# Turning z(1)'s third piece and loading v(1)'s first piece one stage earlier

## The chip, the cores and the metric

The kernel runs on one core of a Trainium2 chip. The metric is the device time of one execution in microseconds. The span in the profile, from the first to the last instruction, is about 1.8 us shorter than that time (916.8 for an execution of 918.57). A timed set is five rounds of one kernel beside the kernel before, on the same chip. Four such sets are used, called the first to the fourth; the second to the fourth ran on three different chips.

In the views, PE is TensorE's matmuls, PEld its weight loads, DVE is VectorE, ACT ScalarE, POOL GpSimd, and SPq the DMA queue that SyncE fills. A transfer has landed when its data is in place. The DMA share is the time of all packets over that of 16 engines; it passes 1 in some stretches here (1.19 from 98 to 104 us in the first trace).

## The reference, cut to what matters

```python
batch, seq, d_model, d_qk, d_ff = 8, 3072, 256, 64, 1024
scores = (1 / seq) * z @ z.T              # per batch
attn   = relu(scores) ** 2
x      = u * (attn @ v)                   # gated attention unit
out    = max(x @ w1, x @ w2) @ w_out      # feed-forward with maxout
```

## The kernel before

Each batch is cut into six groups of 512 rows, and two groups are a couple. For a couple, TensorE runs a stage of products of attention blocks with v. Score pairs for later couples are interleaved with those products. While a couple's gates are prepared, TensorE runs the feed-forward stage ("ff") of the couple before it. All matmuls are bf16.

Scores need z transposed and doubled. A batch's z comes in three pieces of 1,024 rows. Each is loaded (`load_z`), doubled by two VectorE copies, and transposed by a DMA (`turn_z`):

```python
def turn_z(b, piece):
    t = zpool.tile([P, 2 * G, 2, dqk], bf16, name="zd")
    for h in range(2):
        nc.vector.tensor_copy(t[:, :, h, :], zn[b, piece])              # L141, DVE
    nc.sync.dma_start_transpose(                                        # L142, SP queue
        zT[:, ds(z_at(b, piece * 2 * G), 2 * G), :], t.rearrange("p t h d -> p (t h d)"))

def load_v(b, piece, lo=0, n=2 * G, held=False):
    # [cut: takes a tile of the pool of five]
    nc.gpsimd.dma_start(out=t[:, ds(lo, n), :], in_=...)                # L156, POOL queue, 512 KB
```

The place of these calls is set by hand. In batch 0's last couple (`i == 2`, 96 steps, with 22 score pairs of batch 1 interleaved) a plan names the step of each. The ff stage ahead of it takes tasks at fixed places, six in each of its two groups:

```python
# ahead of the couple: the ff stage of batch 0's first couple
second(PLAIN // 2 - 2, [lambda: turn_z(1, 1), lambda: None] + tasks)    # tasks: two gates

if i == 2:
    plan = [
        (2, load_u, 0, 4), (6, load_u, 0, 5),
        (14, turn_z, 1, 2),            # the third piece of z(1)
        (24, load_v, 1, 0),            # the first piece of v(1)
        (52, turn_u, 0, 4), (58, turn_u, 0, 5),
        (len(steps), load_v, 1, 1),
    ]
# the loop over steps (cut)
mm = nc.tensor.matmul(a.out(acc[name]), w()[rows], a.moving(rows, j), ...)   # L880, products
```

The score matmuls are at L210, block transposes (SP queue) at L262, u's transposes (SP queue) at L186.

## Time and profile before

| | before |
|---|---|
| median of the first three timed executions | 914.85 us (914.19 to 915.84) |
| the execution that was profiled | **918.57 us**, span 916.8 us |
| TensorE busy in it | 904.3 us |

The head of the page of the kernel before says that TensorE fills the span:

```profile
span 916.8 us, 19322 instructions
## 1 busy us (share of the span) xinstructions
PE 904.3 (99%) x7518; PEld 519.9 (57%) x7566; DVE 707.8 (77%) x1077; ACT 603.6 (66%) x1192; POOL 105.8 (12%) x199
```

The list of waits of PE (who waited for what: total us, times, longest) leads with the transposed z:

```profile
PE s_ps L210 <- DMA zT<-zd: 2.0, 1, 2.0
PE acc L581 <- DVE blk L557: 1.2, 1, 1.2
```

The timeline of PE shows where (start, duration, what, how many; in brackets the idle time before it and what ended it). Score pairs normally start 1.08 us apart with 8 products between them, 1.29 us with 10:

```profile
97.06 0.38 PE L210 MATMUL s_ps<-zT 64*128 64x512 bf16 x2
97.28 1.03 PE L880 MATMUL acc<-blk,v_sb 64*128 64x512 bf16 x8
100.35 0.39 PE L210 MATMUL s_ps<-zT 64*128 64x512 bf16 x2 [2.04 <-DMA zT<-zd]
100.58 2.04 PE L880 MATMUL acc<-blk,v_sb 64*128 64x512 bf16 x10
102.41 0.64 PE L210 MATMUL s_ps<-zT 64*128 64x512 bf16 x2
```

The pair at 100.35 is the couple's fifteenth, the first that reads z(1)'s third piece. Ten products after it take 2.04 us instead of 1.24. The timeline of the SP queue, and the view of the tile zT in this stretch, show how late the piece was:

```profile
85.76 3.67 SPq L262 DMA_TRANSPOSE blk<-blk  x1
89.53 1.25 SPq L142 DMA_TRANSPOSE zT<-zd  x1
90.87 9.11 SPq L186 DMA_TRANSPOSE uT<-un  x2
...
DMA to landing us min/median/max: 10.8/10.8/10.8
```

Just before its issue, the timeline of POOL has the load of v(1) that flies beside it:

```profile
89.26 0.53 POOL L156 DMA_DIRECT2D v_sb<-in_v_dram  x1 [4.58 <-PE acc L880]
```

Stretches of the same trace (us, then the busy time of PE, PEld, DVE, ACT and POOL, the granted TensorE clock, the DMA share and GB/s) show spare DMA time ahead of the couple, and the halt, with the lowered clock after it:

```profile
74.00:82.00 8.00, 7.95 (x59) 5.46 (x60) 0.00 (x0) 5.10 (x10) 1.09 (x2) 1.00 0.67 110
90.00:98.00 8.00, 8.00 (x78) 3.54 (x74) 4.86 (x8) 7.58 (x16) 0.00 (x0) 1.00 1.14 107
98.00:104.00 6.00, 3.96 (x24) 1.39 (x22) 1.59 (x3) 2.57 (x6) 0.00 (x0) 0.74 1.19 200
```

### The profile page before, as it was taken

How to read it: one execution, taken by the hardware profiler on the slowest of the kernel's cores; microseconds unless marked ns; L12 is line 12 of the kernel's file. 1: busy time of each engine (PE TensorE's matmuls, PEld its weight loads, DVE VectorE, ACT ScalarE, POOL GpSimd, SP SyncE). 2: the span in 40 equal slices, each digit the busy share in tenths (PEclk: the TensorE clock that was granted, in tenths of full speed). 3: DMA queues.
4: the chain of work that ended last, by engine and by line, in shares of the span. 5: the costliest groups of instructions: out<-in, count | busy, mean ns of one | idle time of the engine just before them, and what ended most of it. 6: DMA issues, size and time to landing. Idle time of an engine off the chain costs nothing.

```text
span 916.8 us, 19322 instructions
## 1 busy us (share of the span) xinstructions
PE 904.3 (99%) x7518; PEld 519.9 (57%) x7566; DVE 707.8 (77%) x1077; ACT 603.6 (66%) x1192; POOL 105.8 (12%) x199
## 2 busy tenths in 40 slices
PE   8999999999999999999999999999999999999998
PEld 4456365564655655655556656466465564655655
DVE  6772526888997799987998979979799788995640
ACT  6797756567666676766666666766766667673445
POOL 3101020110101101101011111010110110100000
PEclk9999999999999999999999999999999999999999
DMA  9998999999899897998979999899979999697201
GB/s 184 188 192 159 164 192 137 185 171 162 142 173 187 161 162 139 192 187 141 175 124 207 172 147 168 141 199 161 163 149 162 181 165 174 131 178 140 80 24 69
DMA packets 379499, 145.07 MB, mean 158 GB/s; under 512 B 358160, under 2 KB 362640, under 8 KB 379408
## 3 DMA queue, kind: packets, MB, share of 16 engines
q1 hardware_dynamic: 356960, 91.27, 62.3%
q0 software_dynamic: 22448, 52.57, 29.7%
q8 instruction: 59, 0.97, 0.4%
q14 instruction: 32, 0.26, 0.1%
HBM read 59.77 MB, written 25.17 MB: 93 GB/s over the span
## 4 chain that ended last, share of the span: by engine, by line
PE 96%; DMA 1%; DVE 1%; issue 0%; ACT 0%; ACTq 0%; DVEq 0%
PE acc L880 44%; PE o_ps L462 18%; PE d_ps L439 18%; PE s_ps L210 7%; PE o_ps L453 5%; PE acc L278 4%; DMA zT<-zd 1%; DVE blk L231 1%; PE acc L581 0%; ACT r_sb L223 0%; DVE r_sb L221 0%; PE w2o_ps L673 0%; ACT zT L128 0%; PE tpw L658 0%; DVE xT L423 0%
## 5 line engine op out<-in xcount | busy, mean ns | idle before, releaser
L880 PE MATMUL acc<-blk,v_sb 64*128 64x512 bf16 x2304 | 454.6, 378 | 0.0
L223 ACT ACTIVATE r_sb<-s_ps 128x512 bf16<-128x512 f32 (+3 forms) x668 | 334.3, 558 | 129.1 <-PE s_ps L210 87.3
L880 PE MATMUL acc<-blk,vt 64*128 64x512 bf16 x1440 | 346.7, 376 | 0.0
L880 PEld LDWEIGHTS <-v_sb 64*128 64x128 bf16 x2304 | 178.5, 94 | 139.6 <-issue 7.7
L231 DVE TENSOR_TENSOR blk<-r_sb 128x1024 bf16<-128x1024 bf16 x257 | 173.1, 690 | 109.5 <-ACT r_sb L223 108.4
L446 ACT ACTIVATE g_sb<-d_ps 128x512 bf16<-128x512 f32 x384 | 193.3, 627 | 27.9 <-PE acc L880 17.1
L462 PE MATMUL o_ps<-w_out_sb,g_sb 128*128 128x256 bf16 x1536 | 175.5, 273 | 0.0
L439 PE MATMUL d_ps<-xT,w_sb 128*128 128x512 bf16 x720 | 167.9, 379 | 2.6 <-issue 0.2
L880 PEld LDWEIGHTS <-vt 64*128 64x128 bf16 x1440 | 132.6, 94 | 59.9
L462 PEld LDWEIGHTS <-g_sb 128*128 128x128 bf16 x1536 | 150.3, 98 | 17.4
L474 ACT COPY o_sb<-o_ps 128x512 f32<-128x512 f32 (+1 forms) x98 | 56.4, 578 | 132.1 <-PE o_ps L462 132.1
L210 PE MATMUL s_ps<-zT 64*128 64x512 bf16 (+3 forms) x676 | 126.3, 359 | 2.7 <-DMA zT<-zd 2.0
L439 PEld LDWEIGHTS <-w_sb 128*128 128x128 bf16 x768 | 73.2, 98 | 89.9 <-issue 10.3
L762 DVE TENSOR_TENSOR h_sb<-h_sb,acc 128x512 f32<-128x512 f32 x160 | 104.3, 683 | 23.3 <-ACT h_sb L766 16.0
L475 POOL DMA_DIRECT2D out_dram<-o_sb x88 | 48.2, 547 | 500.7 <-ACT o_sb L474 500.7
L330 DVE TENSOR_TENSOR blk<-blk,blk 128x2048 bf16<-128x2048 bf16 x60 | 73.2, 1219 | 7.3 <-DMA blk<-blk 7.2
L334 DVE TENSOR_TENSOR blk<-blk,blk 128x2048 bf16<-128x2048 bf16 x60 | 73.5, 1225 | 2.0
L777 DVE TENSOR_TENSOR blk<-blk,blk 128x2048 bf16<-128x2048 bf16 x60 | 73.0, 1219 | 0.0
L338 DVE TENSOR_TENSOR blk<-blk,blk 128x2048 bf16<-128x2048 bf16 x60 | 69.8, 1218 | 0.0
L423 DVE SCALAR_TENSOR_TENSOR xT<-h_sb,uT 128x512 bf16<-128x512 f32 x96 | 62.0, 685 | 5.5 <-PE o_ps L453 3.9
L229 DVE TENSOR_TENSOR blk<-r_sb 128x512 bf16<-128x512 bf16 (+3 forms) x162 | 46.3, 323 | 21.2 <-ACT r_sb L223 20.2
L210 PEld LDWEIGHTS <-zT 64*128 64x128 bf16 x676 | 35.7, 94 | 41.2 <-DMA zT<-zd 2.5
(50 smaller groups left out, 322.8 us busy)
## 6 DMA issues: line engine op xcount, KB each, us to landing
out_dram<-o_sb POOLq DMA_DIRECT2D x88, 256.0 KB, 3.6
un<-in_u_dram POOLq DMA_DIRECT2D x48, 256.0 KB, 6.2
v_sb<-in_v_dram POOLq DMA_DIRECT2D x21, 512.0 KB, 7.8
blk<-blk SPq DMA_TRANSPOSE x239, 5.1
zn<-in_z_dram POOLq DMA_DIRECT2D x21, 128.0 KB, 3.7
v_sb<-in_v_dram POOLq DMA_DIRECT2D x6, 256.0 KB, 7.4
out_dram<-o_sb SPq DMA_DIRECT2D x6, 256.0 KB, 2.0
blk<-in_moe_w_dram POOLq DMA_DIRECT2D x2, 512.0 KB, 7.2
```

The costliest lines, as they stand in the source:

```text
L210: nc.tensor.matmul(s_ps[h][:, lo[h] :], zT[rows, z_at(b, blk * G + tiles[h]), :], zT[rows, q + lo[h] // P : q + G, :].rearrange("p t c -> ...
L223: nc.scalar.activation(o, s, AF.Relu)
L231: nc.vector.tensor_mul(a[:, k : k + 2, :], r, r)
L330: nc.vector.tensor_add(*alike(f["S1"], f["A21"], f["A22"]))
L334: nc.vector.tensor_sub(*alike(f["S2"], f["S1"], f["A11"]))
L338: nc.vector.tensor_sub(*alike(f["S3"], f["A11"], f["A21"]))
L439: nc.tensor.matmul(d_ps, w15_sb[:, kc, ts(nb, P)], xT[:, kc, :], start=(kc == 0), stop=(kc == KD - 1),)
L446: nc.scalar.activation(g_sb[:, nb, :], d_ps, AF.Relu)
L462: nc.tensor.matmul(o_ps[t // 2][:, t % 2, :], g_sb[:, nb, ts(t, P)], w_out_sb[:, nb, :], start=False, stop=(nb == KF - 1 and t % 2 == 1),)
L762: nc.vector.tensor_add(out, a, b_)
L777: nc.vector.tensor_sub(f["A12"].ap, f["A12"].ap, f["S2"].ap)
L880: mm = nc.tensor.matmul(a.out(acc[name]), w()[rows], a.moving(rows, j), start=name not in opened, stop=left[name] == 0,)
```

## The change

Both calls move from the couple into the ff stage ahead of it, so that the transpose has landed long before its use and the load of v starts at 75.67 us instead of 89.26.

```diff
-        second(PLAIN // 2 - 2, [lambda: turn_z(1, 1), lambda: None] + tasks)
+        second(
+            PLAIN // 2 - 2,
+            [lambda: turn_z(1, 1)]
+            + tasks
+            + [lambda: turn_z(1, 2)]
+            + [lambda: None] * 2
+            + [lambda: load_v(1, 0)],
+        )
@@ plan of i == 2
-                    (14, turn_z, 1, 2),
-                    (24, load_v, 1, 0),
```

## The prediction

> **What bounds the kernel.** TensorE: 904.3 of 916.8 us busy (page, part 1), and 96% of the chain that ended last is PE. The list of waits gives PE almost nothing to wait for: one wait of 2.0 us on the transposed z (`zT<-zd`), the longest on PE, and scraps of 1.2 us and less, all outside the region of the change. So the whole kernel can win little more than what hangs on that one wait.
>
> **The wait.** In batch 0's last couple (PE from 82 us) 22 score pairs of batch 1 are interleaved; from the fifteenth on they read z(1)'s third piece. In the timeline its doubling copies run on DVE at 85.6, its transpose is issued by SP only at 89.53, behind a 3.67 us block transpose, and lands 10.77 us later; transposes of z take 3.7 us at the median of all 21. It flies beside a 512 KB load of v(1) (issued 89.26, 7.6 us) and u's transposes (from 90.87); the windows show DMA share 1.14 in 90 to 98. PE has done fourteen pairs and stands until 100.35.
>
> **Its full cost.** Score starts before and after: 97.06, then 100.35, 102.41, 104.42. Elsewhere in the same couple such distances are 1.08 us (8 products between) or 1.29 (10). 97.06 to 104.42 is 7.36 us against 1.08 + 1.29 + 1.08 = 3.45: lost 3.91 us. Of it 2.2 us is standing still; 1.7 us is slow matmuls after it (pairs at about 0.42 us apart instead of 0.216, granted clock 0.74 in 98 to 104, 1.00 around it). [...]
>
> **What the change does.** No work is added or removed. By the built order, the two copies (0.49 us on DVE) go ahead of the first block product of that couple, into a stretch (72.0 to 83.9 us) where DVE idles 11.9 us. The transpose follows directly on that of the second piece, so SP issues it at about 74.5 to 76. The load of v goes between the output writes of the first couple's two ff groups; it no longer waits for PE, so starts near 75.7 instead of 89.3. In 74 to 82 the DMA share is 0.67, so there is room. Estimate: with landing between the 3.7 median and 10.8 worst, zT is there by 79 to 87 us, at least 11 us before its use at 98. z(0) is no longer read then, so it is not held up. The second piece (issued 72.4, 6.2 us) may land a few us later, but is first used at 89.1.
>
> **On the critical path:** all 3.91 us, since PE is the chain here and further PE waits on DMA do not follow in the trace. Lighter DMA at 89 to 98 gives nothing more directly: u's transposes come earlier, but nobody waits for them.
>
> **Predicted:** 914.85 - 3.9 = 910.95 us; range 909.7 to 912.9. Faster by over 2%: 0.005; within: 0.99; slower: 0.005.
>
> **Would show it right:** no PE wait on zT; clock 1.00 through the couple; all later PE work shifted about 3.9 us earlier, span near 913; third zT transpose issued near 75. **Wrong:** a PE wait at the fifteenth pair, or slow matmuls, remain.
>
> **What could spoil it:** with PE 3.9 us earlier, block transposes (DMA share about 1.1 to 1.2 from 98 to 128) or u's transposes may turn late for the next stages, handing some back; the early v load may delay the second zT piece past 85 us, moving the stall forward; run spread (914.19 to 915.84) is itself 1.6 us.

## The result, and the profile after

| | before | after |
|---|---|---|
| median of five timed executions | 914.85 us (914.19 to 915.84) | 914.91 us (914.45 to 915.31) |
| ratio of the mean times, 95% interval | | 1.000 (0.9986 to 1.0015) |
| profiled execution | 918.57 us, span 916.8 | 915.31 us, span 913.5 |

A ratio here is the mean time of one kernel's fast runs over that of the other's of the same rounds, so it is not quite the ratio of the medians.

The two profiles differ by 3.3 us in span, the timed executions by nothing. The predicted 910.95 us was wrong, and so was its range of 909.7 to 912.9.

In the trace, nearly every step went as predicted. The head of the page after, and the first line of PE's waits, where the transpose of z (`zT<-zd`) no longer stands. (Each trace also has waits of 0.9 us or less at the start of the kernel for parts of zT that ACT or DVE write; they are left out where this text says "no wait on zT".)

```profile
span 913.5 us, 19368 instructions
...
PE acc L278 <- DVE blk L231: 1.3, 4, 0.6
```

The timelines of POOL, SP and PE after:

```profile
75.67 0.55 POOL L156 DMA_DIRECT2D v_sb<-in_v_dram  x1
...
73.14 4.83 SPq L142 DMA_TRANSPOSE zT<-zd  x2
85.74 5.05 SPq L262 DMA_TRANSPOSE blk<-blk  x1
...
97.09 0.38 PE L210 MATMUL s_ps<-zT 64*128 64x512 bf16 x2
97.30 1.03 PE L885 MATMUL acc<-blk,v_sb 64*128 64x512 bf16 x8
98.17 0.38 PE L210 MATMUL s_ps<-zT 64*128 64x512 bf16 x2
98.38 1.24 PE L885 MATMUL acc<-blk,v_sb 64*128 64x512 bf16 x10
```

The two transposes of z on the SP queue, and the window that showed the halt:

```profile
L142 SPq DMA_TRANSPOSE zT<-zd x2: 1371/2362/3353, 73.1 to 76.6; - x2
DMA to landing us min/median/max: 7.7/8.1/8.5
...
98.00:104.00 6.00, 6.00 (x60) 2.68 (x57) 3.69 (x6) 5.79 (x12) 0.00 (x0) 1.00 1.15 212
```

The third piece is issued at 76.6 and landed by 85.1, 13 us before the fifteenth pair at 98.17. The second piece landed by about 81, before its use at 89.1. From 82 to 112 us PE has no gap, the clock is 1.00, and the next ff stage starts at 107.54 instead of 111.42.

So the trace loses a 3.9 us delay (3.3 us are left of it at the end of the span) and the timed executions lose nothing. Either the trace of before was not of an ordinary execution, or the time came back in a way the trace does not show. That was the question for the experiments.

### The profile page after: what moved, and what is told of

It is laid out like the page before. It is cut to its first block, busy times and chain, and to the rows that moved or that the text cites. A ratio compares the mean times of both kernels' runs of the same rounds, so it can differ in the third digit from the quotient of the medians.

```text
span 913.5 us, 19368 instructions
## 1 busy us (share of the span) xinstructions
PE 905.2 (99%) x7566; PEld 519.5 (57%) x7566; DVE 707.8 (77%) x1077; ACT 603.5 (66%) x1192; POOL 105.4 (12%) x199
## 4 chain that ended last, share of the span: by engine, by line
PE 94%; DVE 3%; DMA 2%; ACT 1%; issue 1%; SPq 0%; POOL 0%; ACTq 0%; DVEq 0%; POOLq 0%
PE acc L885 43%; PE d_ps L439 18%; PE o_ps L462 18%; PE s_ps L210 7%; PE o_ps L453 4%; PE acc L278 4%; DMA uT<-un 2%; DVE blk L231 1%; ACT r_sb L223 0%; DVE xT L423 0%; DVE blk L330 0%; DVE blk L338 0%; PE acc L581 0%; DVE blk L334 0%; DVE r_sb L221 0%
## 5 line engine op out<-in xcount | busy, mean ns | idle before, releaser
L439 PE MATMUL d_ps<-xT,w_sb 128*128 128x512 bf16 x768 | 174.0, 379 | 0.0
```

The lines of the kernel that those rows point to most:

```text
L439: nc.tensor.matmul(d_ps, w15_sb[:, kc, ts(nb, P)], xT[:, kc, :], start=(kc == 0), stop=(kc == KD - 1),)
```

## The experiments

Theory A: the stall belongs to some executions of the kernel before only, and the profile caught one of them. In an ordinary execution the transpose lands just in time. Rival B: every execution has the stall, and the change gives its gain back elsewhere. Rival C came up when slow executions of before appeared: they are slow for some other reason.

All time lists below are in microseconds. "Quiet" means about 914.7, the median of the executions of before below 916 (914.72) and of all executions of the changed kernel (914.68).

### 1. Before, unchanged, traced again (second set)

> The kernel before, unchanged, profiled again. Theory A (the profile of before, 918.57 us, caught a rare late landing of the third z(1) transpose, and the ordinary execution of 914.2 to 915.8 us has no stall there): span near 913, no wait of PE on zT, clock 1.00 throughout the couple, and the execution takes 914 to 916 us. Rival B (every execution of before has that stall, and the changed kernel gives the 3.9 us back elsewhere): PE again waits about 2 us for zT at the fifteenth pair, and the span is 3 us above that of the changed kernel. The timed ratio to before is 1.000 under both, within 0.001.

Its profiled execution took 914.83 us, span 913.1. PE has no wait on zT. The transpose was issued at 89.8, as before, and landed sooner:

```profile
L142 SPq DMA_TRANSPOSE zT<-zd x1: 1250/1250/1250, 89.8 to 89.8; - x1
...
DMA to landing us min/median/max: 8.1/8.1/8.1
```

That is 97.9, and the fifteenth pair starts at 98.35 without a wait. The margin is half a microsecond. Rival B falls: an ordinary execution of before has no stall to give back.

The timed executions had a surprise. In this set before took 914.55, 915.05, 925.26, 914.73, 918.38, 916.29, 917.46, 917.13, 914.48, 923.66 and 914.63, and this copy 914.83, 915.52, 918.55, 915.05, 918.67 and 914.59. The same program has executions at 914.5 and executions 2 to 11 us slower. The ratio of the copy to before was 0.9987 (0.9943 to 1.0030), just outside the 0.001 expected; later copies gave 0.9989 and 0.9985. So a ratio 0.0015 off 1 says nothing in these sets: identical programs give it too.

### 2. Each half of the change alone (same set)

```diff
 only_turn: as the change, but without
-            + [lambda: load_v(1, 0)]
 and with (24, load_v, 1, 0) kept in the plan
```

> The turn of z(1)'s third piece alone moved into the ff stage; the load of v(1) stays at step 24. Theory A: no PE wait on zT, time equal to before within 1 us. Rival B, if the early load of v is what gives the gain back: faster than before by 3 to 4 us (about 911).

```diff
 only_load: as the change, but
-            + [lambda: turn_z(1, 2)]
+            + [lambda: None]
 and with (14, turn_z, 1, 2) kept in the plan
```

> The load of v(1)'s first piece alone moved; the turn stays at step 14. Theory A: time equal to before within 1 us, and the transpose lands no later than before; no PE wait on zT unless a late landing is caught. Rival B: the stall at the fifteenth pair stays if the block transpose ahead delays it, or shrinks if the load of v was its cause.

Moving the turn alone gave 914.38 to 915.13 in six executions; moving the load alone gave 914.39 to 915.06. Ratios to before are 0.9968 each (0.9930 to 1.0005 and 0.9931 to 1.0006). Neither has a slow execution, while before had six of eleven above 916 in the same rounds. With the load gone, the transpose, still issued at 89.85, lands in 4.8 us instead of 8.1, at 94.7. Either half alone left no slow execution in six, and no wait on zT in its trace.

### 3. The turn moved the other way (same set)

```diff
-                    (14, turn_z, 1, 2),
+                    (50, turn_z, 1, 2),      # after load_v(1, 0)
```

> The turn moved the other way, from step 14 to step 50 of the couple, so about 11 us later; its copies then run near 97 us, and the transpose lands near 102 to 105, after its first use at 98.3. Both theories: a PE wait on zT in every execution, of 3 to 7 us, and slow matmuls at half clock after it. If the costs in the prediction are right (stall plus about 1.7 us of slow matmuls), the time is 5 to 9 us above before, 920 to 924 us. If such a stall is hidden or given back later in the kernel, the time stays within 1 us of before.

The test missed. The copies ran at 94.7, not 97, SP issued at 95.24, and the transpose landed in 3.3 us, at 98.5. PE waited 0.22 us. So a transpose issued 5.4 us later than in b_again landed only 0.6 us later. The step of a plan fixes the place in an engine's order, not its time: here step 50 put the copies at 94.7 us, 9.1 us after those of step 14 in the first trace (85.6).

The times were 914.68 to 915.62 and one of 922.05, which was the traced one. That 922.05 lies in the expected 920 to 924 is chance. Its stall was of another transfer, the load of v(1)'s third piece, issued at 127.78 and landed 15.7 us later:

```profile
PE acc L880 <- DMA v_sb<-in_v_dram: 3.9, 1, 3.9
```

### 4. A stall made on purpose (third set)

```diff
-                    (14, turn_z, 1, 2),
+                    (60, turn_z, 1, 2),      # after both turn_u
```

> The turn moved from step 14 to step 60, just before its first use: SP should issue it near 98 and it should land near 101.5, after the need at 98.3 in every execution. If a stall here is paid in full: PE waits 2.5 to 4 us for zT, with up to 1.7 us of slow matmuls after it, time 3 to 6 us above the quiet 914.5 in every execution, 917.5 to 920.5. If it were hidden or given back later (rival B): within 1 us of 914.7.

All six executions were slow: 917.08, 917.4, 919.23, 919.27, 920.41 and 921.65 (three of them outside the expected 917.5 to 920.5), against 914.20 to 918.17 for before in the same rounds (ratio 1.0037, 1.0019 to 1.0056). In the traced one, of 919.23:

```profile
97.16 0.38 PE L210 MATMUL s_ps<-zT 64*128 64x512 bf16 x2
97.37 1.03 PE L880 MATMUL acc<-blk,v_sb 64*128 64x512 bf16 x8
101.06 0.39 PE L210 MATMUL s_ps<-zT 64*128 64x512 bf16 x2 [2.66 <-DMA zT<-zd]
101.29 1.40 PE L880 MATMUL acc<-blk,v_sb 64*128 64x512 bf16 x10
102.48 0.64 PE L210 MATMUL s_ps<-zT 64*128 64x512 bf16 x2
```

The next regular start is at 106.21. From 97.16 that is 9.05 us, where 1.08 + 1.29 + 1.08 + 1.08 = 4.53 are normal: 4.52 us lost, and the execution is 4.5 us above quiet. A stall here is paid in full at the end. The way of costing it in the prediction was sound. (Quiet executions themselves spread from 914.2 to 915.8, so that the two agree so closely is partly luck.)

### 5. More traffic beside the transpose, in both kernels (same set)

```diff
 b_hog (on before) and a_hog (on the changed kernel)
+                    (18, load_v, 1, 1),
-                    (len(steps), load_v, 1, 1),
```

> Before, with the load of v(1)'s second piece (512 KB) pulled from the couple's end to step 18, so that 1 MB of v moves beside the transpose at 89 to 98 instead of 512 KB. Theory A (the transpose waits for loads of v to drain and has only 0.5 us to spare): landing about 4 us later or more, PE waits 2 to 7 us for zT in every execution, time 4 to 9 us above 914.5. Rival C, or a transpose indifferent to loads: time within 1 us of before's lowest.

> The changed kernel with the same load pulled to step 18. Theory A: its zT landed near 82, so nothing on the way to PE waits: no PE wait on zT, 914.2 to 915.5 us, and the ratio of this to b_hog is 0.990 to 0.996, which is the value of the change when DMA is crowded. If instead the crowding itself costs (by u's or the block transposes), this kernel is slowed like b_hog.

On before, the transpose landed in 9.8 us and PE waited 0.92 us in the traced execution (97.19 to 100.66, 3.47 us against 2.37, so 1.10 lost). All six executions lie at 915.82 to 916.41, so here the loss is there every time. I had expected two to seven times as much waiting. The changed kernel with the same load has no wait on zT and took 914.39 to 915.72. The means differ by 1.0 us, 914.99 against 916.02 (a ratio of 0.9989, just outside the 0.990 to 0.996 expected). The direction is as theory A says; the size of the crowding was overestimated. Against before in the same rounds b_hog is no slower (ratio 1.0003, 0.9988 to 1.0018; means 916.02 and 915.63): before has a larger loss in some executions, b_hog a small one in all.

### 6. The changed kernel beside before again (third and fourth set)

> The changed kernel, unchanged, on another chip beside before. Theory A (in a quiet execution of before the transpose lands about 0.5 us before its first use, so the change wins nothing there; only an execution in which DMA is slow just then pays 3 to 11 us, and the change spares it that): lowest times of the two equal within 0.5 us, 914.2 to 914.8; the changed kernel's own executions rarely above 916, those of before sometimes at 917 to 925 if this chip is disturbed; median ratio 0.995 to 1.000. Rival C (the slow executions have nothing to do with this transpose): slow executions come in both kernels equally often.

> The changed kernel again, beside b2, b3 and before on the same chip. Theory A: all executions 914.2 to 915.8, no PE wait on zT. Against before, ratio between 0.995 and 1.000, depending on how often before is stalled on this chip; with no stalled execution of before, 1.000 within 0.0005. Rival C: slow executions as often as in b2 and b3.

In the third set the changed kernel took 914.52 to 914.93 in five executions, and before 914.20 to 918.17, five of eleven above 916. The ratio is 0.9988 (0.9974 to 1.0003). In the fourth it took 914.37 to 915.16 in six, and before 914.40 to 924.59, three of eleven above 916. The ratio is 0.9980 (0.9949 to 1.0010). No interval excludes 1, because before itself scatters. The copies of before, with 0.9985 to 0.9989, show that the ratio cannot tell the kernels apart; the number of slow executions is what differs. No traced execution of the changed kernel has a wait on zT.

### 7. The turn at step 4 (fourth set)

```diff
-                    (14, turn_z, 1, 2),
+                    (4, turn_z, 1, 2),
```

> Before with the turn at step 4 of the same couple instead of 14, nothing else moved: a third way to give the transpose time. Its DVE copies go ahead of that couple's first block product, SP issues it near 84 instead of 89.5, ahead of the block transpose, and it should land near 88 to 92, before the load of v(1) crowds it. Theory A: no PE wait on zT, all executions 914.2 to 915.8, lowest equal to that of before. Rival C: slow executions as often as in before.

I had the issue wrong again. VectorE had nothing to wait for, ran the copies at 72.07, and SP issued the transpose within the 4.27 us that begin at 73.84, far earlier than "near 84". It is the same placement as in only_turn by another edit. Five executions took 914.34 to 914.78 and one 918.92. That one was not traced. Its turn had the same early place, so its slowness probably has another cause, as that of late50 had.

### 8. Six more traces of before

> Before once more, unchanged: more executions and one more profile. Theory A: its executions are again of two kinds, quiet ones at 914.2 to 915 and stalled ones at 916 to 925; if the profiled one is above 916, its trace shows a PE wait on zT at the fifteenth pair, and that wait plus slow matmuls makes up its distance from 914.7 within 0.5 us. Rival C: a profiled execution above 916 with no wait on zT.

> The same again, a further profile: the same readings as for b2.

> Before, one more traced execution. Theory A: if it is above 916 us, PE waits for zT at the fifteenth pair, and the delay read between the score starts around it equals the distance from 914.7 us within 0.5 us; if it is at 914 to 915.5, the transpose landed before 98.4 or within 0.5 us after. Rival C: above 916 us without that wait.

> Before, another traced execution. Theory A: above 916 us only with the PE wait on zT at the fifteenth pair, whose delay accounts for the distance from 914.7 us within 0.5 us. Rival C: above 916 us without that wait.

> Before, another traced execution. Theory A: above 916 us only with the PE wait on zT at the fifteenth pair, whose delay accounts for the distance from 914.7 us within 0.5 us. Rival C: above 916 us without that wait.

> Before, another traced execution. Theory A: above 916 us only with the PE wait on zT at the fifteenth pair, whose delay accounts for the distance from 914.7 us within 0.5 us. Rival C: above 916 us without that wait.

With these six, the first trace and b_again, there are eight traced executions of the same program. "Lost" is the time between score starts from the fourteenth pair to the return of the regular distance, less the regular distances. "Fetch" is the longest packet of the queue that the profile calls "q14 instruction" between 94 and 97 us, from the packet records; it is taken here as a fetch of instructions.

| trace | time | above 914.7 | zT issued | landed after | PE waited | lost | fetch |
|---|---|---|---|---|---|---|---|
| the first | 918.57 | 3.9 | 89.53 | 10.8 | 2.04 | 3.91 | 3.79 |
| b4 | 917.09 | 2.4 | 89.82 | 10.7 | 2.08 | 2.26 | 3.66 |
| b6 | 916.55 | 1.9 | 89.31 | 10.7 | 1.94 | 2.12 | 4.21 |
| b_again | 914.83 | 0.1 | 89.79 | 8.1 | none | 0 | 1.01 |
| b7 | 915.02 | 0.3 | 89.99 | 7.9 | none | 0 | 1.03 |
| b2 | 914.60 | -0.1 | 89.53 | 7.6 | none | 0 | 1.06 |
| b5 | 914.56 | -0.1 | 89.61 | 7.6 | none | 0 | 0.86 |
| b3 | 915.01 | 0.3 | 90.02 | 7.4 | none | 0 | 0.43 |

Theory A holds in all eight. Profiling is not what makes them slow: five of the eight are quiet. Every traced execution of before above 916 has this stall, it accounts for the excess within 0.3 us, and no traced quiet one has it. Rival C falls for these three; it stays open for the untraced executions, above all those above 920.

The timeline of PE in b4 shows the wait without the slow matmuls: the ten products take 1.24 us, and the next pair follows after the regular 1.30.

```profile
97.27 0.38 PE L210 MATMUL s_ps<-zT 64*128 64x512 bf16 x2
97.49 1.03 PE L880 MATMUL acc<-blk,v_sb 64*128 64x512 bf16 x8
100.60 0.39 PE L210 MATMUL s_ps<-zT 64*128 64x512 bf16 x2 [2.08 <-DMA zT<-zd]
100.82 1.24 PE L880 MATMUL acc<-blk,v_sb 64*128 64x512 bf16 x10
101.90 0.38 PE L210 MATMUL s_ps<-zT 64*128 64x512 bf16 x2
```

Why does it land at two times? From 91 to 94 us, the DMA view by queue (packets, MB, share of 16 engines) of the quiet b_again is this; the first trace has the same picture:

```profile
q0 software_dynamic: 93, 0.38, 82.3%
q1 hardware_dynamic: 2, 0.00, 0.1%
```

The load of v (queue q0) runs, and the transposes (queue q1) move next to nothing. In the view from 94 to 96 us, by slices of 0.05 us, the small packets of the transposes set in at 94.4 in b_again (94.2 in the first trace), and the load lands at 95.9 in b_again (98.4 in the first trace). From 95 to 97.5 us the two part. First the quiet b_again, then the first trace:

```profile
DMA packets 1267, 0.33 MB, mean 131 GB/s; under 512 B 1265, under 2 KB 1265, under 8 KB 1266
```

```profile
DMA packets 126, 0.06 MB, mean 22 GB/s; under 512 B 120, under 2 KB 120, under 8 KB 126
```

In the first trace the transposes' small packets all but stop for this stretch, and they resume at 98. In 94 to 96 us lies one packet of the instruction queue, in b_again and then in the first trace:

```profile
q14 instruction: 1, 0.01, 3.2%
```

```profile
q14 instruction: 1, 0.01, 11.8%
```

A share of 11.8% of 16 engines over 2 us is 3.8 us for this one packet, against 1.0 us (3.2%). All three stalled executions have such a packet of 3.7 to 4.2 us, all five quiet ones have only packets of about 1.1 us or less. So late landing and long fetch go together in eight of eight. A long fetch is not needed for a late landing, though: in b_hog the transpose took 9.8 us with a fetch of 0.32.

The load of v was slow as well in the stalled executions. The view of the tile v_sb, from 84 to 104 us, first in the first trace, then in b_again:

```profile
DMA to landing us min/median/max: 9.1/9.1/9.1
```

```profile
DMA to landing us min/median/max: 6.4/6.4/6.4
```

It took 9.1 and 8.9 us in b4 and b6, and 6.0 to 6.5 in the three quiet traces for which it was read (b_again, b5 and b7). So load, fetch and transposes were slow together. Whether the fetch holds up the others, or all are held up by something else, these runs cannot tell: none was made without the fetch.

## Why the prediction was wrong

- **The stall, its place and its cost were read rightly.** The wait on zT, the 3.91 us by score starts, and the fact that all of it is on the path are confirmed by b4, b6 and late60, where the same reckoning meets the time within 0.3 us.
- **What the change does in the trace was right.** No work was added. The load starts at 75.67 (predicted 75.7), the transpose at 76.6 (74.5 to 76), it lands at 85.1 (79 to 87), the wait and the slow clock are gone, and the next stage starts 3.9 us earlier. PE waited for nothing new of weight in exchange: its waits sum to 3.8 us, against 3.7 in the quiet b_again.
- **The step that failed is the line "914.85 - 3.9 = 910.95".** It takes a loss found in one execution off the time of others. The traced execution took 918.57 us; the timed ones, at 914.19 to 915.84, did not have the loss. Off its own execution it would have been 918.57 - 3.9 = 914.7, and the changed kernel's median is 914.91, over all sixteen executions 914.68. The number that gave this away was on hand: the profiled execution was 2.7 us slower than the slowest timed one, and even its span, 916.8 us, is longer than that one's 915.84.
- **A second sign was misread.** The prediction set the 3.7 us median landing of z's transposes beside the 10.8 us of this one. The ordinary landing of this one, beside the load of v, is 7.4 to 8.1 us, which is 0.5 to 1.1 us before its use at 98.1 to 98.6. The 7.6 us that it gives for the load of v is the median of two loads; this one took 9.1.
- **"Run spread" stood among what could spoil it, with 1.6 us**, but as noise, not as the question of which executions have the stall.

What the change is worth is therefore not 3.9 us of every execution. It removes a race that before wins by 0.5 to 1.1 us in the quiet traces and loses in the three stalled ones. Over everything, 21 of 61 timed executions of before (its copies included, the first profiled one not) were above 916, mean 915.99. None of sixteen of the changed kernel was above 915.31, mean 914.73. With the other kernels whose transpose or load was moved ahead (only_turn, only_load, a_hog, turn4), 1 of 39 was above 916. In the third and fourth set, where both ran, before and its copies had 11 slow of 34; had the changed kernel had the same chance, its eleven executions there would all have been quiet with a chance of (23/34) to the 11th, 1.4%. (This takes executions as independent, and the line of 916 was drawn after the times were seen.) In the first set, where none of before's five timed executions was slow, the gain is nil.

What stays open: what makes the fetch, the load and the transposes slow in some executions, and the cause of the 19 slow executions of before that were not traced. One of the longest probably had more than this one stall: at 924.59 us the mean clock was 0.993, so about 6 us of clock were missing (an estimate, 0.007 of its 922.8 us span), where the first trace, with one 3.41 us stretch at half clock (100.88 to 104.29 us), has 0.998.

## What to carry to other kernels

Before taking a stall off a median, check that the profiled execution took the median's time; if it is slower, the difference is the first candidate for what the stall is. For every transfer that feeds the critical engine, compare its landing with its first use: here a margin of 0.5 to 1.1 us, beside a landing that moves between 7.4 and 10.8, was a stall in some executions. Moving the transfer into a stage with idle DMA time (a share of 0.67 from 74 to 82 us before the change) cost nothing here and bought a steadier time rather than a lower best one.

## What the traces show of the clock, the queues and the fetches

- The clock fell after some waits of TensorE and not after others. In the first trace, after the wait of 2.04 us that ended at 100.35, it was at half from 100.88 to 104.29 us (3.41 us; 1.00 on both sides). In late60, after a wait of 2.66 us, and in late50, after one of 3.94, score pairs took 0.64 and 0.65 us instead of 0.38, and the mean clock of the execution was 0.998 and 0.996. After waits of 0.92 (b_hog), 1.94 (b6) and 2.08 us (b4) the ten products took the ordinary 1.24 us and the score pairs 0.38; b4 shows a clock of 1.00 from 98 to 104. So a wait of about 2 us cost either 2.1 to 2.3 us or 3.9 us, and its length alone does not tell which. These are six waits; what decides was not shown, and no run was made to test it.
- From 91 to 94 us b_again shows 93 packets of the software queue and 2 of the hardware one, although transposes had been issued at 89.8 and 91.1. What held them is not shown. A transpose issued beside a 512 KB load landed in 7.4 to 8.1 us in the five quiet traces of before, and one without it in 4.8 (only_load).
- The longest packets of the instruction queue between 94 and 97 us took about 1.1 us or less in five executions of before and 3.7 to 4.2 us in three, and in just those three the transpose landed about 3 us late and TensorE stood still for 1.9 to 2.1 us. That is a coincidence in eight of eight, not a proven cause.
- Executions of this one program on one core fell into two kinds, 914.2 to 915.8 and 916.3 to 925.3 us, and a profile shows one of them.
